# A first expert tile gathered, turned and partly multiplied earlier, inside attention

## Chip, cores and metric

One core of a Trainium2 chip runs the whole program: linear attention, a top-1 mixture of experts (MoE) and a dense gated layer (FFN), in float32. The metric is device time in microseconds (us). The kernel before takes 884.85 us, the median of three runs (881.26 to 886.94).

## What is computed

The reference, cut to its core:

```python
# q, k, v: 4 batches x 8 heads x 576 x 64;  w_phi: 64 x 128
proj = x @ w_phi;  proj = proj - max(abs(proj), -1)
phi(x) = concat(exp(proj), exp(-proj))
kv = phi(k).T @ v;  z = phi(k).sum(2)
attn = (phi(q) @ kv) / (phi(q) @ z + 1e-6)
x = attn as 2304 tokens x 512
e = argmax(x @ w_gate);  g = max softmax(x @ w_gate) * sigmoid(x @ w_output_gate)[e]
x[tokens of e] = g * (relu(x @ w1[e]) @ w2[e])      # 8 experts, 512 -> 1024 -> 512
h = x @ w_in;  out = (h * sigmoid(h)) @ w_out        # 512 -> 2048 -> 512
```

## The kernel before, in words

**Attention** runs in eight units u = 0 to 7, one per pair of heads and half of the tokens (two batches, 1152 tokens, nine tiles of 128). `attention()` writes the order out by hand and the engines keep it: PE (TensorE), DVE (VectorE), ACT (ScalarE) and POOL (GpSimd) execute in that order; only SP's DMA queue is ordered by the scheduler. A unit projects q in three groups (L122), reduces and subtracts the maxima on DVE (L127, L128), adds up kv (L148), copies kv out on ACT (L153), turns q through PSUM (L165) and takes exponentials on ACT (L167, L168), and then attends in three groups g (L184, divided on DVE in L189 to L191), among them the projection of the next unit's k. Small parts are hung in at numbered places n = 0 to 6 of a unit by `other(u, n)`. Units 4 to 7 also load the first expert's weights: the expert that the first half of the tokens chose most often is known in unit 4, and `first_expert(1)` fetches one 128x512 piece into a staging tile `wst` (two rooms), casts it to the high part on ACT (L256) and subtracts for the low part on POOL (L257). There are sixteen pieces, eight each of w1 and w2. All matmuls of the experts and the FFN take a high and a low part of each operand, three matmuls for one product.

**The first tile** is 416 rows of that expert, all of the first half of the tokens. After attention's last q is turned, DVE works out the slots of these tokens (`early_slots`, L465 to L482), nine small matmuls and DVE make a list of tokens (`early_tokens`, L489 to L492), POOL gathers the rows from DRAM (L687) and scales them (L704), and PE turns them (L725) into `xh` and `xl` (L727 ACT, L728 DVE). `gate(1, ...)` meanwhile turns the second half's x (L204), forms logits (L216) and adds them up (L226, L227), and `choose()` picks the experts. PSUM pools in attention: `pj` two tiles of two banks, `pv` one bank, `pm` three.

**The experts.** `Moe.run()` does tile 0 first: eight hidden blocks of twelve matmuls of 416 columns (`first_early`, L789), with the second half's slots (L438 to L441, `route.slots`) after two of them; then `route.tokens` (L489), the gather for tile 1, `route.weights` (some thirty small DVE instructions, L552 to L591), and four output products d = 0 to 3 of 24 matmuls (L826), with `side()` and the turn of tile 1 (L725) after d = 2. Tiles 1 onwards hold 256 rows, or 128 by another branch of the program (`first_small`, L763, `second_small`, L774), depending on how full an expert's last tile is; `way(t, ...)` branches at run time. New expert weights are converted by ACT and DVE (L671, L672) when a tile starts a new expert.

**Side work.** The FFN's weights arrive as float64. Eight of their pieces are converted during the expert tiles, `side_work(i)`: one ACT and six DVE instructions and another ACT and DVE pair (L939 to L970). Before, piece 0 goes into tile 0, pieces 1 and 2 into tile 1, 3 into tile 3, 4 into tile 5, 5 and 6 into tile 6, 7 into tile 7. The FFN follows, on PE alone as its path (L1051, L1072).

Of the kernel before, what the change touches and what calls it, by code (L numbers as in the profile page):

```python
# [21 lines left out]
NF = 128  # L22
# [3 lines left out]
UT = NT // 2  # L26
# [48 lines left out]
def attention(tc, c, k, qT, kT, v, w_phi, w_gate, w_ogate, w1, w2, w, xs, route, early_tile):  # L75
# [5 lines left out]
    xp = c.enter_context(tc.tile_pool(name="a_x", bufs=1))  # L81
    sm = c.enter_context(tc.tile_pool(name="a_s", bufs=4))
    ep = c.enter_context(tc.tile_pool(name="a_e", bufs=1))
    lc = c.enter_context(ExitStack())
    ld = lc.enter_context(tc.tile_pool(name="a_ld", bufs=1))
    pj = c.enter_context(tc.tile_pool(name="a_pj", bufs=2, space=PSUM))
# [25 lines left out]
    def project(u, nm, g):  # L112

        if g == 0:
            st["d" + nm, u] = ep.tile([128, UT, 2, NF], F32, name="d" + nm)
# [12 lines left out]
        V.tensor_tensor(  # L128
            out=d[:, 3 * g:3 * g + 3].rearrange("p t j f -> p j t f"), in0=p, in1=mx.to_broadcast([128, 2, 3, NF]), op=ALU.subtract
        )  # L130

    def exp_k(u, a, z):
        if a == 0:
            st["E", u] = ep.tile([128, UT, 2, 2, NF], F32, name="E")
# [134 lines left out]
    load(0, "k")  # L269
    load(0, "q")  # L270
    load_v(0)
# [5 lines left out]
    for u in range(NU):  # L277
# [24 lines left out]
        kv(u, 1, 1, 1)  # L302
        turn_q(u, 4)
        other(u, 6)
        if u == H // 2 + 1:
            route.ranks(0, pm.tile([128, 512], F32, name="pm"), sm.tile([128, UT * NE], F32, name="rtmp", bufs=1))
        if not last:
            load(u + 1, "q")
            load_v(u + 1)
        else:  # L310
            first_expert(1)
            lc.close()
            tile0 = early_tile()
        for g in range(NG):
            if not last:
                for p in ((0, 1), (), (2,))[g]:
                    project(u + 1, "k", p)
            attend(u, g)
            if not last:
                exp_k(u + 1, 3 * g, 3 * g + 3)  # L320
# [6 lines left out]
            if last:  # L327
                if g < 2:
                    tile0[g](pm)
                else:  # L330
                    tile0[2]()
                gate(1, (0, 3, 10)[g])
# [277 lines left out]
class Moe:  # L610
# [15 lines left out]
    def open(self, c):  # L626
        tc = self.tc
        sp = c.enter_context(tc.tile_pool(name="m_s", bufs=1, reuse_waits="tile"))
        pt, ph, py = (c.enter_context(tc.tile_pool(name=n, bufs=1, space=PSUM, reuse_waits="tile")) for n in ("m_pt", "m_ph", "m_py"))
        self.hh, self.hl = (sp.tile([128, FC, T0], F32R, name=n) for n in ("hh", "hl"))  # L630
        self.y = [sp.tile([128, KC * TW], F32R, name=n) for n in ("yph", "ypl")]
        self.hs = sp.tile([128, FE], F32, name="hs")
        self.turned = self.ring(pt, "pt", [128, 512], 2)
        self.hidden = self.ring(ph, "ph", [128, 2, TW], 4)
        self.result = self.ring(py, "py", [128, 2, TW], 2)
# [148 lines left out]
    def hidden_block(self, p, f, n):  # L784
        nc, w = self.nc, self.w
        for kc in range(KC):
            fs = slice(kc * FE + f * 128, kc * FE + (f + 1) * 128)
            for i, (a, b) in enumerate((("w1h", self.xh), ("w1h", self.xl), ("w1l", self.xh))):
                nc.tensor.matmul(p, w[a][:, fs], b[:, kc, 0:n], start=kc == 0 and i == 0, stop=kc == KC - 1 and i == 2)  # L789

    def first_early(self, blocks):
        nc = self.nc
        for f in blocks:
            p = self.hidden[f % 4].rearrange("p a n -> p (a n)")[:, 0:T0]
            self.hidden_block(p, f, T0)
            h = self.hs[:, f % 2 * 512:f % 2 * 512 + T0]
            nc.scalar.activation(h, p, AF.Relu)
            nc.scalar.copy(self.hh[:, f, :], h)
            nc.gpsimd.tensor_sub(self.hl[:, f, :], h, self.hh[:, f, :].bitcast(F32))

    def first(self, t):
        nc = self.nc
# [25 lines left out]
    def second_early(self, side, turn):  # L828

        banks = [*self.result, *self.hidden[2:4]]  # L830
        for d in range(KC):
            p = banks[d].rearrange("p a n -> p (a n)")[:, 0:T0]
            for f in range(FC):
                self.products(p, f, d, T0, f == 0, f == FC - 1)
            if d == 2:
                side()
                turn()
            self.leave(p.unsqueeze(1), d % 2 * T0)
            self.store(0, slice(d, d + 1), T0, d % 2 * T0)

# [8 lines left out]
    def run(self, route, side_load, side_work, after):  # L849
        tc, nc = self.tc, self.nc  # L850
        side_load(0)
        side_load(1)
        self.first_early((0, 1))
        route.slots(self.turned[0])
        self.first_early(range(2, FC))
        route.tokens(self.turned[1])
        self.gather(1)
        self.scale(1)
        self.gather(2)
        route.weights()  # L860
        self.refill(0, "w1")
        self.new_first(1)

        def side():
            self.refill(0, "w2")
            side_work(0)

        self.second_early(side, lambda: self.turn(1))
# [235 lines left out]
def build(tc, qT, kT, v, w_phi, w_gate, w_ogate, w1, w2, w_in, w_out, out, dbg=None):  # L1104
    nc = tc.nc
    with ExitStack() as c:
# [11 lines left out]
        with ExitStack() as e:  # L1118
            with ExitStack() as m:
# [4 lines left out]
                def early_tile():  # L1124
                    xp = m.enter_context(tc.tile_pool(name="m_x", bufs=1, side="left", reuse_waits="tile"))
                    mo.open_x(xp)
                    route.open(m.enter_context(tc.tile_pool(name="r_s", bufs=1, side="left", reuse_waits="tile")))

                    def tokens(pp):
                        route.early_tokens(pp.tile([128, 512], F32, name="pm"))  # L1130
                        mo.gather_early()

                    def turn(h, pp):
                        mo.turn_early(h, pp.tile([128, 512], F32, name="pm"))

                    return lambda pp: route.early_slots(), tokens, mo.scale_early, turn

                with ExitStack() as a, tc.using_default_side("right"), tc.manual_schedule(engines={ENG.PE, ENG.DVE, ENG.Activation, ENG.Pool}):
                    attention(tc, a, k, qT, kT, v, w_phi, w_gate, w_ogate, w1, w2, w, xs, route, early_tile)
# [105 lines left out]
```

## Time and profile before

| | us |
|---|---|
| median of 3 runs | 884.85 |
| lowest, highest | 881.26, 886.94 |
| the profiled execution: its own time | 886.65 |
| its span, first to last instruction | 884.5 |
| PE busy in the span | 835.2 |
| DVE, ACT, POOL busy | 503.4, 359.8, 151.6 |

A row of a timeline gives the start in the span, the duration, engine, line, operation, what it writes and reads, how many were merged, and in brackets the idle time just before it with what ended it. PE's loads of weights overlap its matmuls. Matmuls are pipelined, so 0.35 us of one matmul is a latency, and the time between two starts is what it costs.

### The profile page before, as it was taken

How to read it: one execution, taken by the hardware profiler on the slowest of the kernel's cores; microseconds unless marked ns; L12 is line 12 of the kernel's file. 1: busy time of each engine (PE TensorE's matmuls, PEld its weight loads, DVE VectorE, ACT ScalarE, POOL GpSimd, SP SyncE). 2: the span in 40 equal slices, each digit the busy share in tenths (PEclk: the TensorE clock that was granted, in tenths of full speed). 3: DMA queues.
4: the chain of work that ended last, by engine and by line, in shares of the span. 5: the costliest groups of instructions: out<-in, count | busy, mean ns of one | idle time of the engine just before them, and what ended most of it. 6: DMA issues, size and time to landing. Idle time of an engine off the chain costs nothing. (4 is left out here: it accounts for less than half of the span.)

```text
span 884.5 us, 19046 instructions
## 1 busy us (share of the span) xinstructions
PE 835.2 (94%) x7812; PEld 763.8 (86%) x7812; DVE 503.4 (57%) x872; ACT 359.8 (41%) x641; POOL 151.6 (17%) x139
## 2 busy tenths in 40 slices
PE   7999998789889999998998999999999999999997
PEld 6888787669878989988998999999999999999996
DVE  5777577447666867666253888888423323232322
ACT  4556566443346665225153545544222222222220
POOL 0000024446422322201260101000002101010001
PEclk9999999999989999999999999999999999999999
DMA  4444356333857798326552855731023120210000
GB/s 143 150 131 127 91 167 186 91 101 106 311 176 250 264 295 301 122 74 210 151 162 83 236 168 168 225 107 49 1 72 100 44 72 36 55 41 13 6 31 36
DMA packets 59217, 113.96 MB, mean 129 GB/s; under 512 B 7056, under 2 KB 47120, under 8 KB 57312
## 3 DMA queue, kind: packets, MB, share of 16 engines
q1 hardware_dynamic: 42640, 81.10, 28.6%
q0 software_dynamic: 16464, 31.33, 12.5%
q8 instruction: 75, 1.23, 0.6%
q14 instruction: 38, 0.31, 0.1%
HBM read 91.79 MB, written 20.62 MB: 127 GB/s over the span
## 5 line engine op out<-in xcount | busy, mean ns | idle before, releaser
L1054 DVE TENSOR_TENSOR g<-fph,g 128x384 f32<-128x384 f32 x96 | 53.5, 557 | 150.8 <-ACT g L1053 150.5
L1053 ACT ACTIVATE g<-fph 128x384 f32<-128x384 f32 x96 | 47.2, 492 | 199.0 <-PE fph L1051 198.9
L789 PE MATMUL ph<-xh,w1h 128*128 128x256 f32 (+1 forms) x256 | 75.1, 293 | 2.2 <-DVE lg L227 1.1
L1055 ACT CAST gh<-g 128x384 fp32r<-128x384 f32 x96 | 49.4, 514 | 64.7 <-DVE g L1054 64.7
L789 PE MATMUL ph<-xh,w1l 128*128 128x256 f32 (+1 forms) x256 | 74.7, 292 | 0.0
L789 PE MATMUL ph<-xl,w1h 128*128 128x256 f32 (+1 forms) x256 | 74.5, 291 | 0.0
L826 PE MATMUL py<-hh,w2h 128*128 128x256 f32 (+1 forms) x240 | 69.9, 291 | 4.6 <-ACT hh L807 3.0
L1058 DVE TENSOR_TENSOR gl<-g,gh 128x384 fp32r<-128x384 f32 x96 | 53.4, 557 | 36.5 <-ACT gh L1055 36.5
L826 PE MATMUL py<-hl,w2h 128*128 128x256 f32 (+1 forms) x240 | 69.1, 288 | 0.7 <-DVE hl L808 0.7
L826 PE MATMUL py<-hh,w2l 128*128 128x256 f32 (+1 forms) x240 | 69.1, 288 | 0.0
L1051 PE MATMUL fph<-yh,i0h 128*128 128x384 f32 x192 | 65.6, 342 | 0.7 <-PEq L908 0.7
L1051 PE MATMUL fph<-yh,i0l 128*128 128x384 f32 x192 | 65.4, 341 | 0.0
L1051 PE MATMUL fph<-yl,i0h 128*128 128x384 f32 x192 | 65.1, 339 | 0.0
L127 DVE TENSOR_REDUCE pmx<-pj 128x6 f32<-128x768 f32 x48 | 45.6, 949 | 32.8 <-PE pj L122 32.8
L985 POOL DMA_DIRECT2D yh<-yTh x12 | 9.3, 776 | 281.3 <-PE fph L1051 228.7
L704 POOL TENSOR_SCALAR xg<-xg 128x512 f32<-128x512 f32 (+1 forms) x28 | 52.4, 1878 | 27.5 <-DMA xg<-xs,tok 27.3
L1072 PE MATMUL fpo<-o0l,gh 128*128 128x512 f32 x144 | 57.0, 396 | 0.0
L1072 PE MATMUL fpo<-o0h,gh 128*128 128x512 f32 x144 | 56.7, 394 | 0.0
L1072 PE MATMUL fpo<-o0h,gl 128*128 128x512 f32 x144 | 56.7, 394 | 0.0
L122 PE MATMUL pj<-wphi,raw 64*64 64x128 f32 x1152 | 44.6, 292 | 10.3 <-PE pj L122 5.3
L789 PEld LDWEIGHTS ph<-xh,w1h 128*128 128x128 f32 x256 | 48.9, 191 | 3.2 <-issue 2.2
L826 PEld LDWEIGHTS py<-hh,w2h 128*128 128x128 f32 x240 | 46.0, 192 | 5.5 <-ACT hh L807 3.2
(267 smaller groups left out, 2172.5 us busy)
## 6 DMA issues: line engine op xcount, KB each, us to landing
w1s<-in_w SPq DMA_DIRECT2D x7, 2048.0 KB, 8.1
w2s<-in_w SPq DMA_DIRECT2D x7, 2048.0 KB, 9.5
yh<-yTh POOLq DMA_DIRECT2D x12, 768.0 KB, 5.0
yl<-yTl POOLq DMA_DIRECT2D x12, 768.0 KB, 7.7
raw<-in_w_in SPq DMA_DIRECT2D x16, 512.0 KB, 5.6
raw<-in_w_out SPq DMA_DIRECT2D x16, 512.0 KB, 3.6
v<-in_v SPq DMA_DIRECT2D x8, 650.0 KB, 3.9
raw<-in_k SPq DMA_DIRECT2D x24, 192.0 KB, 4.3
```

The source lines that it names most:

```text
L122: nc.tensor.matmul(ps[c:c + 64, j, i * 128:(i + 1) * 128], t[h, i * 128 + c:i * 128 + c + 64], wphi[h, :], start=True, stop=True)
L127: V.tensor_reduce(mx, p, AX.X, ALU.max, apply_absolute_value=True)
L704: self.nc.gpsimd.tensor_scalar(x[:, 0:DM], x[:, 0:DM], x[:, DM:DM + 1], None, op0=ALU.mult)
L789: nc.tensor.matmul(p, w[a][:, fs], b[:, kc, 0:n], start=kc == 0 and i == 0, stop=kc == KC - 1 and i == 2)
L826: self.nc.tensor.matmul(p, self.w[a][:, fs], b[:, f, 0:n], start=start and i == 0, stop=stop and i == 2)
L985: self.nc.gpsimd.dma_start(out=y, in_=yT[:, :, ch * CN:(ch + 1) * CN])
L1051: nc.tensor.matmul(p, a[:, kc, fs], b[:, kc, :], start=kc == 0 and n == 0, stop=kc == KC - 1 and n == 2)
L1053: nc.scalar.activation(g, p, AF.Sigmoid)
L1054: V.tensor_mul(g, p, g)
L1055: nc.scalar.copy(gh, g)
L1058: V.tensor_sub(gl, g, gh.bitcast(F32))
L1072: nc.tensor.matmul(p, a[:, s], b[:, f, :], start=q < 2 and f == 0 and n == 0, stop=done and n == 2)
```

## The change

The first tile's slots are worked out in unit 5 at n = 3, its list of tokens and its gather stand at n = 6 of unit 5, its scaling at n = 1 of unit 6, and its four turns at n = 0 to 3 of unit 7; `route.ranks` moves from behind unit 5's n = 6 to its n = 0. Hidden block 0 is put ahead of the last unit's attend groups and blocks 1, 2 and 3 among the gate steps behind them; the blocks write to `pj` tiles. `wst` gets four rooms. `dk` and `E` move to a pool that is closed before the last attend, where the hidden tiles are then placed. In tile 0, `route.tokens` and the gather follow product d = 0, `route.weights` follows d = 1, side work and the turn of tile 1 follow d = 2. Side pieces now go: 0 in tile 0, 1 in tile 1, 2 in tile 3, 3 in tile 5, 4 and 5 in tile 6, 6 and 7 in tile 7.

```diff
@@ attention()
-            t = sm.tile([128, 512], F32, name="wst", bufs=2)
+            t = sm.tile([128, 512], F32, name="wst", bufs=4)
...
+        if u == H // 2 + 1:
+            if n == 0:
+                st["tile0"] = early_tile(pm)
+                route.ranks(0, pm.tile([128, 512], F32, name="pm"), sm.tile([128, UT * NE], F32, name="rtmp", bufs=1))
+            elif n == 3:
+                st["tile0"].slots()
+            elif n == 6:
+                st["tile0"].tokens()
         if u > H // 2 and n in (1, 3, 5, 6):
             first_expert(1)
+        if u == H // 2 + 2 and n == 1:
+            st["tile0"].scale()
+        if (u, n) in TURNS:
+            st["tile0"].turn(TURNS.index((u, n)))
...
+    TURNS = [(NU - 1, n) for n in range(4)]
...
-    tile0[3](0, pm)
-    tile0[3](1, pm)
-    gate(1, 1)
-    tile0[3](2, pm)
-    tile0[3](3, pm)
...
+    st["tile0"].open()
+    block(0)
+    for g in range(NG):
+        attend(u, g)
+        first_expert(1)
+    store_x(bp, hp * 128, st["x", bp][:, :, hp * 128:(hp + 1) * 128])
+    gate(1, 6)
+    block(1)
+    gate(1, 8)
+    block(2)
     gate(1, 1)
     decide(1)
+    block(3)
@@ Moe.run()
-        self.first_early((0, 1))
         route.slots(self.turned[0])
-        self.first_early(range(2, FC))
-        route.tokens(self.turned[1])
-        self.gather(1)
-        self.scale(1)
-        self.gather(2)
-        route.weights()
...
+        self.first_early(range(FC // 2, FC))
+
+        def between(d):
+            if d == 0:
+                route.tokens(self.turned[1])
+                self.gather(1)
+                self.scale(1)
+                self.gather(2)
+            elif d == 1:
+                route.weights()
+                self.refill(0, "w1")
+                self.new_first(1)
+            elif d == 2:
+                self.refill(0, "w2")
+                side_work(0)
+                self.turn(1)
...
             if t == 1:
                 side_work(1)
-                side_work(2)
...
-            for i in {3: (3,), 5: (4,), 6: (5, 6), 7: (7,)}.get(t, ()):
+            for i in {3: (2,), 5: (3,), 6: (4, 5), 7: (6, 7)}.get(t, ()):
```

On DVE at the end of attention, the kernel before had the slots of the first tile (`slot` to `rr`) between two groups of the last attend (`den`, `x`):

```order
L191 TENSOR_TENSOR x<-pm,den 128x3x128
L465 CAST slot<-rank 128x9
L468 TENSOR_SCALAR hi<-slot 128x9
L469 TENSOR_SCALAR lo<-slot 128x9
L473 TENSOR_TENSOR mlo<-lo,col 128x1152
L501 TENSOR_TENSOR eq_2851<-hi,tcol 128x36
L502 TENSOR_TENSOR eq_2851<-eq_2851,oh 128x36
L481 TENSOR_SCALAR rr_2852<-eq_2851,row 128x9x4
L482 TENSOR_TENSOR rr_2852<-eq_2851,tcol 128x9x4
L189 TENSOR_SCALAR den<-pm 128x6
```

In the changed kernel the same eight stand in unit 5 behind the last subtraction for q (`dq`), with the list of tokens (`tok`) behind them and unit 6's first k (`pmx`, `dk`) next:

```order
L130 TENSOR_TENSOR dq<-pj,pmx 128x2x3x128
L482 CAST slot<-rank 128x9
L485 TENSOR_SCALAR hi<-slot 128x9
L486 TENSOR_SCALAR lo<-slot 128x9
L490 TENSOR_TENSOR mlo<-lo,col 128x1152
L518 TENSOR_TENSOR eq_2023<-hi,tcol 128x36
L519 TENSOR_TENSOR eq_2023<-eq_2023,oh 128x36
L498 TENSOR_SCALAR rr_2024<-eq_2023,row 128x9x4
L499 TENSOR_TENSOR rr_2024<-eq_2023,tcol 128x9x4
L508 COPY tokf_2193<-pm 128x8
L509 SCALAR_TENSOR_TENSOR tok_96<-tokf_2193 128x4
L129 TENSOR_REDUCE pmx<-pj 128x6
```

The eight have left the last attend and stand two units earlier.

On PE in unit 7, between the projections of q (`pj<-wphi,raw`) and the turns of q (`pm<-ident,dq`), before:

```order
L148 MATMUL pv<-v_2511,E 64x130 x2
L148 MATMUL pv<-v_2511,E 64x65 x16
L148 MATMUL pv<-v_2511,E 64x130 x2
L148 MATMUL pv<-v_2511,E 64x65 x16
L122 MATMUL pj<-wphi,raw 64x128 x12
L148 MATMUL pv<-v_2511,E 64x130 x2
L148 MATMUL pv<-v_2511,E 64x65 x8
L165 MATMUL pm<-ident,dq 128x128 x8
```

and now, with the turns of the first tile's rows (`pm<-ident,xg`) among them:

```order
L150 MATMUL pv<-v_2555,E 64x65 x8
L743 MATMUL pm<-ident,xg 128x128 x4
L150 MATMUL pv<-v_2555,E 64x65 x8
L150 MATMUL pv<-v_2555,E 64x130 x2
L150 MATMUL pv<-v_2555,E 64x65 x8
L743 MATMUL pm<-ident,xg 128x128 x4
L150 MATMUL pv<-v_2555,E 64x65 x8
L124 MATMUL pj<-wphi,raw 64x128 x12
L743 MATMUL pm<-ident,xg 128x128 x4
L150 MATMUL pv<-v_2555,E 64x130 x2
L150 MATMUL pv<-v_2555,E 64x65 x8
L167 MATMUL pm<-ident,dq 128x128 x8
```

Three turns of 128 rows stand ahead of the first turn of q, and the fourth (32 rows) behind it.

On ACT at the start of tile 1, before, two side pieces (`mag`, `i0h`) stand ahead of the tile's own results (`hh`):

```order
L939 ACTIVATE mag<-raw 128x512
L966 CAST i0h<-val 128x512
L939 ACTIVATE mag<-raw 128x512
L966 CAST i0h<-val 128x512
L638 TENSOR_LOAD full
L880 COMPARE_AND_BRANCH
L807 ACTIVATE hh<-ph_3168 128x2x256
```

and now one:

```order
L959 ACTIVATE mag<-raw 128x512
L986 CAST i0h<-val 128x512
L656 TENSOR_LOAD full
L900 COMPARE_AND_BRANCH
L827 ACTIVATE hh<-ph_3234 128x2x256
```

The second pair has gone to tile 3's side piece and so on, up to tile 7, which now has two.

## Rows read from the trace of the kernel before

**Rows 1.** The page: busy us, share of the span, instructions of each engine.

```profile
PE 835.2 (94%) x7812; PEld 763.8 (86%) x7812; DVE 503.4 (57%) x872; ACT 359.8 (41%) x641; POOL 151.6 (17%) x139
```

**Rows 2.** Windows: length, PE, PEld, DVE, ACT, POOL busy, granted clock, DMA share, GB/s.

```profile
170.00:180.00 10.00, 6.09 (x77) 5.25 (x77) 3.67 (x13) 2.77 (x5) 5.82 (x6) 0.83 0.30 86
```

**Rows 3.** Timeline of PE, unit 6's attend and attention's end.

```profile
146.73 3.10 PE L184 MATMUL pm<-kv,eq 128*64 128x65 f32 x96
...
166.05 2.79 PE L184 MATMUL pm<-kv,eq 128*64 128x65 f32 x88 [1.31 <-ACT kv L153]
171.82 0.38 PE L489 MATMUL pm<-rr,mlo 128*128 128x8 bf16 x9 [2.99 <-DVE rr L482]
172.06 2.60 PE L204 MATMUL pm<-ident,x 128*128 128x128 f32 x12
174.59 2.40 PE L184 MATMUL pm<-kv,eq 128*64 128x65 f32 x48
...
180.06 0.85 PE L216 MATMUL pm<-xT,wg 128*32 128x384 f32 x8 [2.04 <-DVE x L191]
...
189.28 0.43 PE L789 MATMUL ph<-xh,w1h 128*128 128x416 f32 x1 [1.11 <-DVE lg L227]
```

**Rows 4.** Waits of PE: us in total, times, longest us.

```profile
PE pv L148 <- ACT kv L153: 2.3, 2, 1.2
```

**Rows 5.** Timelines of DVE, ACT, POOL and SP's queue in units 5 to 7 and after.

```profile
126.10 0.23 DVE L449 TENSOR_TENSOR rtmp<-pm,oh 128x72 f32<-128x72 f32 x1 [3.35 <-PE pm L441]
...
168.38 0.99 DVE L465 CAST slot<-rank 128x9 int32<-128x9 f32 x1
...
158.14 0.62 ACT L256 CAST w2h<-wst 128x512 fp32r<-128x512 f32 x1 [2.30 <-DMA wst<-in_w]
...
173.23 1.16 POOL L687 DMA_INDIRECT xg<-xs,tok  x1 [3.89 <-DVE tok L492]
...
178.12 6.21 POOL L704 TENSOR_SCALAR xg<-xg 128x512 f32<-128x512 f32 x4
...
146.01 0.43 SPq L109 DMA_DIRECT2D v<-in_v  x1
```

**Rows 6.** Groups by line: the first tile's turns on PE (busy us, mean ns).

```profile
L725 PE MATMUL pm<-ident,xg 128*128 128x128 f32 (+1 forms) x16 | 2.0, 263 | 0.2 <-issue 0.2
```

**Rows 7.** Timeline of PE, tile 0 from the slots to tile 1.

```profile
194.51 0.44 PE L789 MATMUL ph<-xh,w1h 128*128 128x416 f32 x1
...
208.20 0.70 PE L489 MATMUL pt<-rr,mlo 128*128 128x64 bf16 x18
...
227.74 0.28 PE L789 MATMUL ph<-xh,w1h 128*128 128x256 f32 x1
```

**Rows 8.** Timeline of DVE, tile 0: list of tokens, weights, side piece, turn.

```profile
208.93 0.23 DVE L491 COPY tokf<-pt 128x64 f32<-128x64 f32 x1 [3.28 <-PE pt L489]
...
216.75 0.23 DVE L591 TENSOR_SCALAR coff<-coff,taken 128x16 int32<-128x16 f32 x1
...
219.14 0.43 DVE L949 TENSOR_SCALAR mag<-mag 128x512 f32<-128x512 f32 x1
...
224.78 1.29 DVE L728 TENSOR_TENSOR xl<-pt,xh 128x512 fp32r<-128x512 f32 x2 [0.44 <-ACT xh L727]
```

**Rows 9.** Timeline of PE and ACT, tiles 1 to 4.

```profile
240.79 0.62 ACT L966 CAST i0h<-val 128x512 fp32r<-128x512 f32 x1 [4.49 <-DVE val L963]
...
242.93 0.38 PE L826 MATMUL py<-hh,w2h 128*128 128x256 f32 x1 [2.95 <-ACT hh L807]
...
260.58 0.47 PE L763 MATMUL ph<-w1h,xh 128*128 128x512 f32 x1 [3.62 <-ACT w2h L671]
...
277.92 0.38 PE L789 MATMUL ph<-xh,w1h 128*128 128x256 f32 x1 [0.19 <-issue]
...
301.40 0.39 PE L763 MATMUL ph<-w1h,xh 128*128 128x512 f32 x1
```

**Rows 10.** DMA queues from 257 to 259 us: packets, MB, share of 16 engines.

```profile
q8 instruction: 1, 0.02, 2.7%
```

More of the change, by code (lines that the diff above doesn't have):

```diff
@@ L83, in attention @@
     ep = c.enter_context(tc.tile_pool(name="a_e", bufs=1))
+    kc = c.enter_context(ExitStack())
+    ek = kc.enter_context(tc.tile_pool(name="a_k", bufs=1))
     lc = c.enter_context(ExitStack())
@@ L114, in project @@
         if g == 0:
-            st["d" + nm, u] = ep.tile([128, UT, 2, NF], F32, name="d" + nm)
+            st["d" + nm, u] = (ek if nm == "k" else ep).tile([128, UT, 2, NF], F32, name="d" + nm)
         d, t = st["d" + nm, u], st.pop(("raw", nm, u, g))
@@ L133, in exp_k @@
         if a == 0:
-            st["E", u] = ep.tile([128, UT, 2, 2, NF], F32, name="E")
+            st["E", u] = ek.tile([128, UT, 2, 2, NF], F32, name="E")
         E, d = st["E", u], st["dk", u]
@@ L304, in attention @@
         other(u, 6)
[L305 to L310, printed above, removed]
+        if last:
             first_expert(1)
             lc.close()
-            tile0 = early_tile()
+            kc.close()
+            break
+        load(u + 1, "q")
+        load_v(u + 1)
         for g in range(NG):
-            if not last:
-                for p in ((0, 1), (), (2,))[g]:
-                    project(u + 1, "k", p)
+            for p in ((0, 1), (), (2,))[g]:
+                project(u + 1, "k", p)
             attend(u, g)
-            if not last:
-                exp_k(u + 1, 3 * g, 3 * g + 3)
+            exp_k(u + 1, 3 * g, 3 * g + 3)
             if u == H // 2 and g == 1:
@@ L326, in attention, with block @@
                 gate(0, 2)
[L327 to L332, printed above, removed]
-        store_x(bp, hp * 128, st["x", bp][:, :, hp * 128:(hp + 1) * 128])
-    tile0[3](0, pm)
-    tile0[3](1, pm)
-    gate(1, 1)
-    tile0[3](2, pm)
-    tile0[3](3, pm)
+        store_x(bp, hp * 128, st["x", bp][:, :, hp * 128:(hp + 1) * 128])
+    def block(f):
+        if f % 2 == 0:
+            st["free"] = pj.tile([128, 2, 512], F32, name="pj")
+        st["tile0"].block(f, st["free"][:, f % 2, 0:T0])
+    st["tile0"].open()
[8 more added lines that the diff above has]
+    block(2)
     gate(1, 1)
     decide(1)
+    block(3)
 def choose(nc, sp, k, lg, route, bp, scale):
@@ L624, in open_x, with open_s @@
         self.xh, self.xl = (sp.tile([128, KC, T0], F32R, name=n) for n in ("xh", "xl"))
[L626 to L629, printed above, removed]
+    def open_s(self, sp):
         self.hh, self.hl = (sp.tile([128, FC, T0], F32R, name=n) for n in ("hh", "hl"))
@@ L632, in open @@
         self.hs = sp.tile([128, FE], F32, name="hs")
+    def open(self, c):
+        tc = self.tc
+        pt, ph, py = (c.enter_context(tc.tile_pool(name=n, bufs=1, space=PSUM, reuse_waits="tile")) for n in ("m_pt", "m_ph", "m_py"))
         self.turned = self.ring(pt, "pt", [128, 512], 2)
@@ L789, in hidden_block, with block_early @@
                 nc.tensor.matmul(p, w[a][:, fs], b[:, kc, 0:n], start=kc == 0 and i == 0, stop=kc == KC - 1 and i == 2)
+    def block_early(self, f, p):
+        nc = self.nc
+        self.hidden_block(p, f, T0)
+        h = self.hs[:, f % 2 * 512:f % 2 * 512 + T0]
+        nc.scalar.activation(h, p, AF.Relu)
+        nc.scalar.copy(self.hh[:, f, :], h)
+        nc.gpsimd.tensor_sub(self.hl[:, f, :], h, self.hh[:, f, :].bitcast(F32))
     def first_early(self, blocks):
-        nc = self.nc
         for f in blocks:
[L794 to L799, printed above, removed]
+            self.block_early(f, self.hidden[(f + 2) % 4].rearrange("p a n -> p (a n)")[:, 0:T0])
     def first(self, t):
@@ L826, in products, with second_early @@
             self.nc.tensor.matmul(p, self.w[a][:, fs], b[:, f, 0:n], start=start and i == 0, stop=stop and i == 2)
-    def second_early(self, side, turn):
+    def second_early(self, between):
         banks = [*self.result, *self.hidden[2:4]]
@@ L834, in second_early @@
                 self.products(p, f, d, T0, f == 0, f == FC - 1)
-            if d == 2:
-                side()
-                turn()
+            between(d)
             self.leave(p.unsqueeze(1), d % 2 * T0)
@@ L852, in run @@
         side_load(1)
-        self.first_early((0, 1))
         route.slots(self.turned[0])
-        self.first_early(range(2, FC))
-        route.tokens(self.turned[1])
-        self.gather(1)
-        self.scale(1)
-        self.gather(2)
-        route.weights()
[L861 to L868, printed above, removed]
+        self.first_early(range(FC // 2, FC))
[13 more added lines that the diff above has]
+                self.turn(1)
+        self.second_early(between)
         def one(t):
@@ L1122, in build, with __init__, pool, bank @@
                 mo = Moe(tc, k, r, w, {"w1": w1, "w2": w2}, xs, yT)
[L1124 to L1130, printed above, removed]
-                        mo.gather_early()
-                    def turn(h, pp):
-                        mo.turn_early(h, pp.tile([128, 512], F32, name="pm"))
-                    return lambda pp: route.early_slots(), tokens, mo.scale_early, turn
+                class Early:
+                    def __init__(self, pp):
+                        self.pp = pp
+                        mo.open_x(self.pool("m_x"))
+                        route.open(self.pool("r_s"))
+                    def pool(self, name):
+                        return m.enter_context(tc.tile_pool(name=name, bufs=1, side="left", reuse_waits="tile"))
+                    def bank(self):
+                        return self.pp.tile([128, 512], F32, name="pm")
+                    def slots(self):
+                        route.early_slots()
+                    def tokens(self):
+                        route.early_tokens(self.bank())
+                        mo.gather_early()
+                    def scale(self):
+                        mo.scale_early()
+                    def turn(self, h):
+                        mo.turn_early(h, self.bank())
+                    def open(self):
+                        mo.open_s(self.pool("m_s"))
+                    def block(self, f, p):
+                        mo.block_early(f, p)
                 with ExitStack() as a, tc.using_default_side("right"), tc.manual_schedule(engines={ENG.PE, ENG.DVE, ENG.Activation, ENG.Pool}):
-                    attention(tc, a, k, qT, kT, v, w_phi, w_gate, w_ogate, w1, w2, w, xs, route, early_tile)
+                    attention(tc, a, k, qT, kT, v, w_phi, w_gate, w_ogate, w1, w2, w, xs, route, Early)
                 ep = e.enter_context(tc.tile_pool(name="f_e", bufs=1, side="right", reuse_waits="tile"))
```

## The prediction

> **What bounds the kernel now.** I read the page first: PE is busy for 835.2 of 884.5 us, 94% of the span [rows 1], so a change pays only where PE stands still or runs slowly, or where it moves that. The FFN at the end is a closed row of matmuls that the change doesn't touch; it starts earlier by whatever PE gains before it. Then I went through the windows of 10 us for places where PE's busy time falls: in 170 to 180 us it is 6.09 of 10, and the granted clock 0.83 [rows 2]. The timeline of PE there names the waits one by one [rows 3]: 1.31 for the last kv copy, 2.99 for the slots' `rr` on DVE, 2.04 behind the last attend, 1.11 for the last logits before the first hidden block; in sum 7.45 us. [...] The second place is tile 1: from 227.74 [rows 7] to the end of its work, 3.62 before 260.58, are 29.2 us, while tile 3, with the same matmuls, takes 301.40 - 277.92 = 23.5 [rows 9]. Between them stands a wait of 2.95 for ACT's `hh`, and ACT was busy with a side piece: its `i0h` of 240.79 had itself waited 4.49 for DVE [rows 9]. Last, PE stands 3.62 before tile 2, at a branch.
>
> **Part by part, against the profiled execution** (886.65 us, 1.8 above the median of the runs shown).
>
> *End of attention.* The chain of slots, list, gather, scale and turn leaves it. Hidden block 0 (one block costs (208.20 - 194.51)/6 = 2.28 us [rows 7]) covers the 1.31; the 2.99 is gone with the slots; blocks 1 and 2 stand where PE waited for the logits' copies; block 3 stands ahead of the second half's slots while `choose` finds the experts. The blocks themselves are only moved. So 7.45 of waits, 1.95 of slow clock, 2.0 of turns [rows 6] and the 0.24 of the list's matmuls (171.82 to 172.06 [rows 3]) leave: 11.6. Against it: three `pm` rooms serve nine turns of x, and ACT now copies them between the blocks' `relu` and cast, which are ahead of the copies in its queue; and DVE must have `choose` done within one block where it had two. The trace before doesn't show that interleaving. Bounds are 0 (each copy lies beside a block) and 3.7, half of the waits there were; I take 1.0, nearer to nothing because a block is longer than any of the copies. Net -10.6, between -11.6 and -7.9.
>
> *Units 5 to 7, which receive the chain.* Slots: 168.38 to 171.82 on DVE, 3.4 us [rows 5, 3], and, as an estimate from the 0.24 of the nine matmuls, some 0.8 with the two DVE instructions behind and the handing over. DVE has 3.35 idle at that place of unit 5 [rows 5], so 0.9 comes out, and what is late is unit 6's first k; bounds 0 and 3.4. Turns: 2.0 on PE in unit 7, which has little idle time; four `xl` on DVE go into a queue that is full there, and the fourth turn needs the `pm` room that the third `xl` frees behind the last subtraction for q: +0.8, bounds 0 and 2. Staging: twice, in units 6 and 7, PE waits for the kv copy, 2.3 together [rows 4], and ACT stood just before that copy in a cast that waited 2.30 for the `wst` DMA [rows 5]; with four rooms that DMA is issued some pieces ahead, so -2.3 (bounds -2.3 and 0). Gather and scale are POOL time, about 4.9 (173.23 to 178.12) and 6.2 [rows 5], beside pieces of w1 and w2 that now have four rooms; I cost them at nothing. If that cover were gone, SP's queue would be late; that is the third rival. Sum +1.4, between -0.3 and +7.4.
>
> *Tile 0.* From the list's matmuls to tile 1, 208.20 to 227.74, are 19.5 us [rows 7]: 0.6 for the list, about 1.0 for the turn of two row blocks, four products of 4.5. Now product 0 goes ahead of the list, so four blocks and one product (13.7) cover the slots' DVE chain, as six blocks (13.7) did; but only 15.0 are left between list and tile 1. DVE's work in that stretch isn't less: from 208.93 to the end of `xl` at 226.07 [rows 8], that is up to 17.9 after the list's matmuls began: the weights' small instructions until 217, the side piece from 219.14, then `xl`. An instruction or two of waiting for ACT falls away, so 17.5. Tile 1's second matmul needs `xl`; PE waits 2.5 us there, where it waited for nothing. Behind this `xl` stand the products' `ypl` and then side piece 1. Bounds: 0, if the changed order lets DVE start early, and 4.5, one product. A wait of 2.99 was followed by the slow clock [rows 3]; half of 1.95 is put down for that, +1.0.
>
> *Tile 1.* One side piece instead of two: DVE is done with it before tile 1's first results are all there, the 2.95 goes, and with it the slow stretch behind. What takes its place is tile 3's shape: 23.5 instead of 29.2, -5.7; bounds -5.7 and -3.0 (the wait alone). The piece goes to tile 3 in exchange for another, and at the end tile 7 gets one more; tiles 3 and 7 have the same matmuls and DVE idle beside them, so nothing.
>
> *Tile 2's branch:* unchanged. The row names ACT's `w2h` as what ended it [rows 9], but in tile 4 the same matmul starts without a wait though the same conversion runs; in 257 to 259 us one packet of instructions is fetched [rows 10]. So I read it as the fetch of the branch's code, which the change doesn't move. [...]
>
> Sum: -10.6 + 1.4 + 2.5 + 1.0 - 5.7 = -11.4. 886.65 - 11.4 = 875.25; taken off the median instead, 884.85 - 11.4 = 873.4, which is the forecast.
>
> **Rivals.** *First, the branch too.* If the fetch comes in time, as in tile 4, another 3.62 and a slow stretch like the 1.95 go: 873.4 - 5.6 = 867.8. For it: tile 4; against it: the same code is reached in the same way.
>
> *Second, DVE becomes the bound.* Every link that leaves PE's end of attention lands in DVE's queue in units 5 and 7, and tile 0 gives it 4.5 us less. If the slots come out whole (+2.5 more), the turns' `xl` by their bound (+1.2 more) and the chain before tile 1 by 4.5 (+2.0 more), 5.7 are given back: 879.1, within 1%. For it: DVE is busy through most of each unit; against it: the idle 3.35 stands right where the slots are put.
>
> *Third, slower, by SP's queue.* SP issues in order, a `wst` load only when POOL has freed a room, and unit 7's v (issued at 146.01 [rows 5]) stands behind such loads. The gathers and scales put 4.9 + 6.2 = 11.1 in front of POOL's pieces. If nothing of that were hidden, PE would stand for 11.1 in units 6 and 7 and run slowly after it (1.95): 873.4 + 13.0 = 886.4, slower than before. It decides if v is issued later than about 150 us; four rooms and two units between them speak against it.
>
> **How the numbers follow.** Forecast as summed 0.57 (its own range 870 to 877), branch too 0.13, DVE 0.25, SP's queue 0.05. The bounds of the parts would allow 862 to 885; nearly all of that at the ends needs several together, so 866 to 880 holds 8 in 10. About 1%, 8.85 us, is what a measurement tells from no change: faster than 876.0 are most of the first case and the second, 0.68; slower than 893.7 only an SP queue worse than priced, 0.03; the rest 0.29.
>
> **What would show it.** Right: no wait of PE for `rr` or for `lg` before the first block; no kv wait of about 1.1 in units 6 and 7; the first FFN matmul some 11 us earlier; tile 1 at about 24 us, with a wait of 2 to 3 for `xl` or `xh` just before it; tile 2's 3.6 still there. Wrong: gaps of PE in units 5 to 7 that end on DVE or on a DMA for v, k or q; waits for ACT's `xT` or `lt` among the gate steps of more than 3 in sum; tile 1's start less than 4 us earlier than 227.74.

## The result and the profile after

The changed kernel takes 873.71 us, the median of four runs (872.32 to 875.18), beside 885.89 for the kernel before on the same chip: ratio 0.9883, 95% interval 0.9858 to 0.9909, faster by 1.2%. A second measurement, below, gave 0.990 (0.9867 to 0.9934), 8.4 us by its medians. The forecast was 873.4 us.

In the profiled execution PE's busy time fell by 5 us [rows 1], and the window in which the kernel before did 6.09 us of work at a clock of 0.83 [rows 2] is nearly full. The page's line, and the window (length, busy time of PE, PEld, DVE, ACT, POOL, granted clock, DMA share, GB/s):

```profile
PE 830.3 (95%) x7812; PEld 758.6 (87%) x7812; DVE 503.9 (58%) x872; ACT 359.1 (41%) x641; POOL 149.4 (17%) x139
```

```profile
170.00:180.00 10.00, 9.39 (x127) 8.02 (x123) 2.52 (x8) 5.03 (x10) 1.17 (x2) 1.00 0.20 62
```

Two marks of the kernel before, from PE's timeline: unit 7's last turns of q, and the FFN's first matmul.

```profile
163.90 0.44 PE L165 MATMUL pm<-ident,dq 128*128 128x128 f32 x2
...
475.56 0.41 PE L1051 MATMUL fph<-yh,i0h 128*128 128x384 f32 x1 [0.73 <-PEq L908]
```

The same marks in the changed kernel, and between them what answers to [rows 3, 7, 9]: waits among the gate steps, the second half's slots (L455), the list (L506), tile 1's first two matmuls, tile 2's first.

```profile
165.04 0.44 PE L167 MATMUL pm<-ident,dq 128*128 128x128 f32 x2
...
173.28 1.50 PE L206 MATMUL pm<-ident,x 128*128 128x128 f32 x12 [0.15 <-DVE x L193]
...
179.68 0.66 PE L206 MATMUL pm<-ident,x 128*128 128x128 f32 x4 [0.46 <-ACT xT L209]
...
186.40 0.45 PE L807 MATMUL pj<-xh,w1h 128*128 128x416 f32 x1 [0.34 <-ACT hs L813]
188.78 0.50 PE L455 MATMUL pt<-oh,ones 128*128 128x80 bf16 x9
...
203.06 0.70 PE L506 MATMUL pt<-rr,mlo 128*128 128x64 bf16 x18
...
218.21 0.38 PE L807 MATMUL ph<-xh,w1h 128*128 128x256 f32 x1
219.34 0.38 PE L807 MATMUL ph<-xl,w1h 128*128 128x256 f32 x1 [0.74 <-DVE xl L746]
...
247.06 0.76 PE L781 MATMUL ph<-w1h,xh 128*128 128x512 f32 x1 [4.21 <-ACT w2h L689]
...
461.94 0.60 PE L1071 MATMUL fph<-yh,i0h 128*128 128x384 f32 x1 [0.72 <-PEq L928]
```

Read as differences, the 13.6 us between the two FFN rows split so: +1.1 up to the turns of q (165.04 against 163.90), made of +1.8 in units 5 to 7 (63.3 us from unit 4's last turn of q, at 101.78, instead of 61.5 from 102.40) and -0.6 ahead of them, where the change does nothing; -9.6 from there to tile 1 at work (219.34 - 165.04 = 54.3, where the kernel before needed 227.74 - 163.90 = 63.8, with 0.1 to its second matmul); -5.7 in tile 1 (219.34 to 242.85, which is 4.21 before 247.06: 23.5 us instead of 29.2); +0.6 at tile 2's branch (4.21 instead of 3.62); the rest up to the FFN is equal within 0.1 (214.88 and 214.98 us).

### The profile page after: what moved, and what is told of

Same layout as the page of the kernel before. It is cut to its first block, busy times and chain, and to the rows that moved or that the text cites. A ratio compares the mean times of both kernels' runs of the same rounds, so it can differ in the third digit from the quotient of the medians.

```text
span 870.8 us, 19045 instructions
## 1 busy us (share of the span) xinstructions
PE 830.3 (95%) x7812; PEld 758.6 (87%) x7812; DVE 503.9 (58%) x872; ACT 359.1 (41%) x641; POOL 149.4 (17%) x139
## 5 line engine op out<-in xcount | busy, mean ns | idle before, releaser
L807 PE MATMUL ph<-xh,w1h 128*128 128x256 f32 (+1 forms) x240 | 68.8, 287 | 1.2 <-ACT yph L840 0.7
L807 PE MATMUL ph<-xl,w1h 128*128 128x256 f32 (+1 forms) x240 | 68.3, 285 | 0.7 <-DVE xl L746 0.7
L807 PE MATMUL ph<-xh,w1l 128*128 128x256 f32 (+1 forms) x240 | 68.3, 284 | 0.0
L722 POOL TENSOR_SCALAR xg<-xg 128x512 f32<-128x512 f32 (+1 forms) x28 | 49.8, 1785 | 31.1 <-DMA xg<-xs,tok 31.0
L124 PEld LDWEIGHTS pj<-wphi,raw 64*64 64x64 f32 x1152 | 34.3, 142 | 16.3 <-issue 7.4
L150 PEld LDWEIGHTS pv<-v,E 128*64 128x64 f32 x1152 | 40.9, 140 | 7.7 <-issue 6.7
```

The costliest lines, as they stand in the source:

```text
L124: nc.tensor.matmul(ps[c:c + 64, j, i * 128:(i + 1) * 128], t[h, i * 128 + c:i * 128 + c + 64], wphi[h, :], start=True, stop=True)
L150: nc.tensor.matmul(pv[f:f + 64, s, o:o + n], E[:, i, j, s, f:f + 64], v1[:, c:c + n], start=i == 4 and s == 0, stop=i == 8 and s == 1,)
L722: self.nc.gpsimd.tensor_scalar(x[:, 0:DM], x[:, 0:DM], x[:, DM:DM + 1], None, op0=ALU.mult)
```

## Experiments

Ratios are to the kernel before, run beside each; 0.001 is 0.9 us. Where nothing else is said, a difference to the changed kernel is taken to 0.9883; to its second ratio, 0.990, it is 1.5 us smaller.

**The pieces, both ways.** In the changed kernel, put back:

```diff
             if t == 1:
                 side_work(1)
+                side_work(2)
-            for i in {3: (2,), 5: (3,), 6: (4, 5), 7: (6, 7)}.get(t, ()):
+            for i in {3: (3,), 5: (4,), 6: (5, 6), 7: (7,)}.get(t, ()):
```

> The changed kernel with the FFN pieces where they stood before (tile 1 converts pieces 1 and 2 again). My theory (term D of the sum): tile 1 is held up by the second piece alone, so its 23.5 to 24.6 us go back to about 29 and the whole is 5.7 us slower than the changed kernel, about 879.4 us, with a wait of PE for hh of about 3 us in tile 1 and a stretch at the lower clock behind it. Rival: tile 1 became shorter because DVE's queue ahead of it is different now, and the piece is harmless: 0 to 2 us slower.

Measured 0.9944 (0.9921 to 0.9966), 5.4 us over the changed kernel's 0.9883. PE's timeline:

```profile
233.00 0.56 PE L846 MATMUL py<-hh,w2h 128*128 128x256 f32 x1 [3.21 <-ACT hh L827]
...
250.32 0.77 PE L781 MATMUL ph<-w1h,xh 128*128 128x512 f32 x1 [2.21 <-ACT w2h L689]
```

The wait for `hh` is back, and tile 1 takes 30.6 us from its second matmul. Two of the 7.0 lost there don't count, because tile 2's wait shrinks from 4.21 to 2.21. The opposite edit, in the kernel before:

> The kernel before with only the FFN pieces moved as in the change. My theory: the term D stands by itself, so tile 1 falls from 29.2 to 23.5 us and the whole is 5.7 us faster than before (ratio about 0.9936). Rival: the wait for hh in tile 1 is tied to before's order of tile 0, and goes only in part: 0 to 3 us.

Measured 0.9946 (0.9924 to 0.9967), 4.8 us faster than before.

```profile
225.13 0.28 PE L789 MATMUL ph<-xh,w1h 128*128 128x256 f32 x1
...
252.56 0.77 PE L763 MATMUL ph<-w1h,xh 128*128 128x512 f32 x1 [3.90 <-ACT w2h L671]
...
270.96 0.38 PE L789 MATMUL ph<-xh,w1h 128*128 128x256 f32 x1 [0.18 <-issue]
```

Tile 1 takes 23.5 us here too. Tile 2's wait is 0.3 longer and its work 1.1 (18.4 against 277.92 - 260.58 = 17.3 [rows 9]). So the term stands by itself, about 5 us after what tile 2 takes back.

**Staging rooms.**

```diff
-            t = sm.tile([128, 512], F32, name="wst", bufs=4)
+            t = sm.tile([128, 512], F32, name="wst", bufs=2)
```

> The changed kernel with two staging rooms instead of four. My theory (part of term A): PE waits again for the kv copy behind ACT's cast, twice about 1.1 us, so +2.3 us against the changed kernel (about 876). Rival one: the chain of gather and scale in front of POOL's pieces makes it worse with two rooms, v of unit 7 is issued late and PE stands for it: +5 or more. Rival two: the waits had gone for another reason, as the order of the casts: 0.

Measured 0.995 (0.9928 to 0.9971): 5.9 us over 0.9883, 4.4 over 0.990. ACT's cast stands in unit 6 for its DMA, PE behind it for the copy, and then PE runs at a granted clock of 0.50 (timelines of ACT and PE, and a window):

```profile
138.69 0.62 ACT L258 CAST w1h<-wst 128x512 fp32r<-128x512 f32 x1 [1.96 <-DMA wst<-in_w]
```

```profile
139.64 0.91 PE L150 MATMUL pv<-v,E 128*64 128x130 f32 x20 [2.44 <-ACT kv L155]
```

```profile
140.60:144.00 3.40, 3.40 (x36) 3.07 (x38) 0.00 (x0) 2.39 (x5) 3.40 (x4) 0.50 0.59 197
```

The mechanism is the one of [rows 4, 5], with its whole weight in unit 6 and a slow stretch that I hadn't priced: 2.44 and some 1.7, an estimate (half of the 3.40 at 0.50). The first half of my first rival holds too: POOL issues the gather until 131.57, frees rooms with its next two pieces until 134.09, and only at 134.12 does SP issue the load that this cast waits for. Its second half doesn't: no gap of PE in units 6 and 7 ends on v. Then both small edits, alone, in the kernel before:

> The kernel before with the two small edits alone: four staging rooms and the FFN pieces moved, nothing of tile 0's chain. My theory: the two terms add up, -2.3 (kv copies in units 6 and 7) and -5.7 less the 0.3 to 1.3 that the kernel before with the pieces alone gave back at tile 2: -6.7 to -8.0 us against before, ratio 0.991 to 0.9925, more than half of the whole change's gain. Rival: the kv waits of the kernel before aren't due to the staging rooms (there nothing but the pieces is in POOL's queue): -4.4 to -5.7.

Measured 0.9916 (0.9896 to 0.9936), 7.4 us faster than before. No wait for the kv copy is left in units 6 and 7, while the end of attention is as it was:

```profile
164.54 2.79 PE L184 MATMUL pm<-kv,eq 128*64 128x65 f32 x88 [1.30 <-ACT kv L153]
169.49 0.38 PE L489 MATMUL pm<-rr,mlo 128*128 128x8 bf16 x9 [2.17 <-DVE rr L482]
```

In this profile units 5 to 7 take 61.4 us, as before (61.5): two pauses of PE with nothing waited for, 2.33 before 114.99 (0.88 at that place in the kernel before) and 1.43 before 151.41, stand against the kv waits that went. So what the rooms give in this kernel rests on the ratios, whose intervals overlap (this run's and the one with the pieces alone).

Two edits of a line or two give most of the whole gain. The long one, tile 0's chain and order, adds some 1.5 to 3 us to them by the ratios, which isn't clear of noise (0.9896 to 0.9936 overlaps both intervals of the changed kernel), though 9.6 leave the stretch from the turns of q to tile 1; the last section has a place where some of that is lost.

**Blocks or chain.** The chain stays in units 5 to 7, the four blocks go back behind attention:

```diff
-    block(0)
...
-    gate(1, 6)
-    block(1)
-    gate(1, 8)
-    block(2)
-    gate(1, 1)
+    gate(1, 15)
     decide(1)
-    block(3)
@@ Moe.run()
+        self.first_early((0, 1))
         route.slots(self.turned[0])
-        self.first_early(range(FC // 2, FC))
+        self.first_early(range(2, FC))
```

> The changed kernel with hidden blocks 0 to 3 of tile 0 back behind attention (0 and 1 ahead of the second half's slots, as before), so only the chain of slots, list, gather, scale and turns stays in units 5 to 7. My theory (term B split in two): the wait of 2.99 us for rr, the slow stretch behind it (1.95), the turns (2.0) and the list's 0.24 stay gone, because they belong to the chain; what the four blocks cover comes back: 1.31 for the kv copy, 2.04 behind the last attend, 1.11 for the logits, 4.5 us in sum, less the 0.95 of small new waits that the interleaving brought: +3.5 us against the changed kernel, and up to 1.95 more if one of the waits is followed by the lower clock. Rival: without the slots in its queue DVE is through with the gate's steps early, and the blocks cover nothing: 0 to 1 us.

Measured 0.9901 (0.988 to 0.9921), no different from the changed kernel. PE's timeline:

```profile
167.48 0.44 PE L167 MATMUL pm<-ident,dq 128*128 128x128 f32 x2
...
169.43 4.19 PE L186 MATMUL pm<-kv,eq 128*64 128x65 f32 x136 [1.13 <-ACT kv L155]
174.79 1.50 PE L206 MATMUL pm<-ident,x 128*128 128x128 f32 x12 [0.15 <-DVE x L193]
...
182.54 0.55 PE L228 MATMUL pm<-ident,lt 128*128 128x128 f32 x3 [0.65 <-ACT lt L220]
187.47 0.50 PE L449 MATMUL pt<-oh,ones 128*128 128x80 bf16 x9
...
222.52 0.38 PE L801 MATMUL ph<-xl,w1h 128*128 128x256 f32 x1 [0.82 <-DVE xl L740]
```

From the turns of q to tile 1 at work are 55.0 us, 0.7 more than with the blocks. Only the 1.31 for the kv copy came back (as 1.13); the 2.04 behind the last attend is 0.15, and the 1.11 for the logits hasn't returned, only 0.65 at an earlier step. So these two waits weren't for lack of other work on PE. DVE's rows of the kernel before show what they were:

```profile
178.93 0.17 DVE L189 TENSOR_SCALAR den<-pm 128x6 f32<-128x6 f32 x1 [6.01 <-PE pm L204]
...
187.98 0.89 DVE L728 TENSOR_TENSOR xl<-pm,xh 128x512 fp32r<-128x512 f32 x2 [0.79 <-ACT xh L727]
188.79 0.35 DVE L227 TENSOR_REDUCE lg<-pm 128x48 f32<-128x192 f32 x1
```

The last `lg` (the 1.11) stood in DVE's queue behind the first tile's `xl`. The last attend's `den` (the 2.04) had itself waited for PE, which had the list's matmuls and twelve turns of x ahead of that attend [rows 3]; in the changed kernel and in this run all gate steps stand behind the attends. The slots' instructions account for the 2.99. My theory fell and the rival holds, though not by the slots only; moving the gate steps wasn't tried by itself.

**Tile 0's order.** The list, weights and first conversion ahead of the products again, as before:

```diff
+        route.tokens(self.turned[1])
+        self.gather(1)
+        self.scale(1)
+        self.gather(2)
+        route.weights()
+        self.refill(0, "w1")
+        self.new_first(1)
         def between(d):
-            if d == 0:
...
-            elif d == 2:
+            if d == 2:
```

> The changed kernel with tile 0's list, weights and first conversion ahead of the four products, as before, while four blocks stay in attention. My theory (term C): the slots' chain on DVE, which one block more than four has to cover (13.7 us of PE's work in either kernel), is covered by 9.1 us only, so PE waits up to 4.5 us at the list's matmuls and may run slowly behind it; in exchange the 0.74 us for xl before tile 1 goes. In sum +3 to +6 us against the changed kernel. Rival: DVE is through with the slots earlier than that, and the list may stand anywhere: 0 to 1 us, or a little faster than the changed kernel because nothing waits for xl.

Measured 0.9927 (0.9907 to 0.9946). PE waits once, and not for `xl`:

```profile
201.29 0.68 PE L506 MATMUL pt<-rr,mlo 128*128 128x64 bf16 x18 [2.09 <-DVE rr L499]
```

From the slots to tile 1 at work that is 1.1 us more than in the changed kernel's profile (189.27 to 220.94, against 188.78 to 219.34), so the wait came at half of its 4.5, and the stage is near my rival's 0 to 1. The ratio says 3.9 us (2.4 to 0.990). The FFN starts 3.1 us later: 0.5 of that comes ahead of the turns of q, and 1.7 behind tile 2's start, where the granted clock is 0.50 in 388.40 to 391.80, which the changed kernel's first profile hasn't there. So the ratio isn't the price of the order alone. The list could start 11.4 us after the slots' matmuls (9.3 of blocks and the wait), sooner than the 13.7 that I took as its cover. Then the turn ahead of the piece:

```diff
+                self.turn(1)
                 side_work(0)
-                self.turn(1)
```

> The changed kernel with the turn of tile 1's rows ahead of the FFN piece in tile 0 instead of behind it. My theory (term C): the 0.41 to 0.82 us that PE waits for xl before tile 1 is DVE's queue alone, in which the piece (4.95 us) stands ahead of xl; with xl first the wait goes and the piece lies beside product 3 and tile 1: -0.4 to -0.8 us, nothing new in tile 1. Rival: the piece now delays the yph and ypl of product 3 and, in ACT's and DVE's queues, tile 1's first hidden results, so PE waits for hh or hl in tile 1 as it did in the kernel before: +1 to +4 us.

Measured 0.9878 (0.9854 to 0.9903), no different from the changed kernel.

```profile
218.89 0.28 PE L807 MATMUL ph<-xh,w1h 128*128 128x256 f32 x1
...
247.83 0.77 PE L781 MATMUL ph<-w1h,xh 128*128 128x512 f32 x1 [5.41 <-ACT w2h L689]
```

The wait for `xl` is gone and tile 1 takes 23.5 us, but tile 2's wait grew from 4.21 to 5.41: from the slots to tile 2 it is 58.3 us in either kernel. What is gained ahead of that branch is partly waited away at it.

**Tile 2's branch.** Matmuls that never execute, in the branch for small tiles of tile 1 (36 or 72), move the rest of PE's program. The changed kernel ran beside them:

```diff
     def first_small(self, t):
+        if t == 1:
+            for _ in range(36):
+                nc.tensor.matmul(...)
```

> The changed kernel itself, as the yardstick on the chip of the other three: the same waits as in its first profile (0.74 for xl before tile 1, about 4.2 at tile 2's branch, 1.5 at tile 8's), and a ratio to before of about 0.988.

Measured 0.990 (0.9867 to 0.9934), with 0.41 for `xl`, 4.84 at tile 2 and 1.91 at tile 8.

> The changed kernel with 36 matmuls added to the branch of tile 1 for small tiles, which isn't taken here: nothing more is executed, but all of PE's program behind it lies 72 instructions later. My theory (term E): the wait before tile 2 is the fetch of the branch's code. PE passes a prefetch hint for the branch one stage ahead of it, and the wait comes where, between hint and branch, the program goes over from one instruction packet to the next (a packet is 16.4 KB in the rows: 1.23 MB in 75). [...] With 36 matmuls more it is so for 2, 4 and 8: the 4.2 and 1.5 stay and tile 4 gets a wait of 2 to 4 us, so 2 to 4 us slower than the changed kernel. [...] Rival: the wait is for ACT's w2h, as the row names it: then no wait changes in any of the three shifts, and the time is the changed kernel's.

Measured 0.9901 (0.9868 to 0.9934).

```profile
246.64 0.39 PE L784 MATMUL ph<-w1h,xh 128*128 128x512 f32 x1
...
290.13 0.77 PE L784 MATMUL ph<-w1h,xh 128*128 128x512 f32 x1 [4.16 <-ACT w2h L689]
```

> As the run before, with 72 matmuls in the branch that isn't taken (144 instructions). By the same count hint and branch of tiles 2 and 8 now lie in one packet and those of tile 4 don't: my theory expects no wait at tile 2 (4.2 before) and tile 8 (1.5), and one of 2 to 4 us at tile 4; in sum -1.5 to -3.5 us against the changed kernel, and another 1.7 (a stretch of 3.4 us at half the clock) if the lower clock behind tile 2's wait goes and none comes behind tile 4's. Rival (ACT's w2h): nothing changes.

Measured 0.989 (0.9859 to 0.9921).

```profile
246.04 0.39 PE L784 MATMUL ph<-w1h,xh 128*128 128x512 f32 x1
...
386.98 0.36 PE L795 MATMUL py<-w2h,hh 128*128 128x256 f32 x1 [3.43 <-ACT w1h L689]
...
450.85 0.47 PE L784 MATMUL ph<-w1h,xh 128*128 128x512 f32 x1 [2.79 <-ACT w2h L689]
```

> Unexecuted matmuls in three places (72 in tile 1's branch for small tiles, 40 and 80 in the branches of tiles 2 and 4 for full ones, none of which is taken here), so that by my count hint and branch lie in one packet for tiles 2, 4 and 8. My theory expects none of the three waits: -4.2 - 1.5 = -5.7 us against the changed kernel, or -7.4 with the stretch at the lower clock, about 866 to 868 us where the changed kernel takes 873.7. Rival (ACT's w2h): nothing changes. A second rival: a branch that is taken costs its wait at some other tile whatever the places are, then 0 to -3.

Measured 0.9929 (0.9908 to 0.9951).

```profile
256.87 0.38 PE L795 MATMUL py<-w2h,hh 128*128 128x256 f32 x1 [2.80 <-ACT w1h L689]
...
298.12 0.38 PE L795 MATMUL py<-w2h,hh 128*128 128x256 f32 x1 [2.37 <-ACT w1h L689]
```

ACT does the same work in all four, yet the wait leaves tile 2 and goes to tile 4, to tile 8's second stage (1.75 of these 3.43 is a wait for DVE that the changed kernel has too) and the last small tile, or to the second stage of tiles 2 and 4 (with 72, another 1.74 stands inside tile 2's second stage). (That last small tile is tile 11; the expectations call it 12.) So it hangs on where PE's code lies and not on `w2h`: the row names what came last, not what was waited for. The DMA records of the traces bear this out. In all ten executions that wait at tile 2, one packet of instructions (16 KB) starts 2.6 to 2.8 us before PE goes on (at 244.31 in the changed kernel, PE at 247.06), and so it does at tile 4 with 36 (287.51, PE at 290.13). In the four that don't wait at tile 2, the last packet started 3.7 to 8.5 us ahead of it (with 36 at 242.96, PE at 246.64). My count of the places was wrong (with 36, tile 2 should have waited). The last attempt took the place without a wait for each tile from these runs:

```diff
     def first_small(self, t):
+        for _ in range({1: 36, 3: 36, 7: 120}.get(t, 0)):
+            nc.tensor.matmul(...)
```

> The changed kernel with unexecuted matmuls in the branches for small tiles of tiles 1, 3 and 7 (36, 36 and 120, none taken here), which gives tile 2 the place in the program that it had with 36 (no wait seen there), tile 4 the one that it had with 72 (none there), and tiles 8 and 12 those of the three-place run. My theory now, after three shifts in which the waits changed their places but not their sum (6.8 and 7.2 us in the changed kernel, 6.9, 7.6 and 10.7 with the shifts, counted as waits at small tiles with nothing but a branch, an issue gap or a converted weight behind them): the sum can't be placed away; it will be 5 to 8 us again, at other places, and the time within 2 us of the changed kernel. Rival: each branch's wait hangs on its own place alone: nothing at tiles 2 and 4, 1.3 + 2.3 at 8, 1.8 at 12, so 5.4 us or less, and 1.5 to 2 us faster than the changed kernel.

Measured 0.9838 (0.9811 to 0.9865), the lowest ratio of all.

```profile
244.41 0.39 PE L783 MATMUL ph<-w1h,xh 128*128 128x512 f32 x1
...
378.07 1.06 PE L743 MATMUL pt<-ident,xg 128*128 128x128 f32 x8 [1.35 <-issue]
385.84 0.58 PE L794 MATMUL py<-w2h,hh 128*128 128x256 f32 x1 [1.52 <-issue]
...
454.03 0.43 PE L794 MATMUL py<-w2h,hh 128*128 128x256 f32 x1 [2.70 <-issue]
```

Tiles 2 and 4 start without a wait, as in the runs from which their places were taken, so there a branch's wait hangs on its own place. At tiles 8 and 11 the places were those of the three-place run, and the waits weren't the same: 1.52 inside tile 8's second stage for 2.31, and 2.70 in tile 11's second stage for 1.81 in its first. The place alone doesn't fix every wait. The waits that are left make 5.6 us, against 6.8 in the changed kernel (4.21, 1.51 and 1.10). The ratio is some 0.005 lower, more than that explains; it wasn't measured beside the changed kernel, and the intervals overlap a little (0.9858 to 0.9865). It beats the kernel before clearly and the changed one probably, for data that fill the tiles as here.

## Why the prediction was right, step by step

By parts, forecast and measured in the profiles: end of attention -10.6 and -10.8, units 5 to 7 +1.4 and +1.8, tile 0 +3.5 and +1.2, tile 1 -5.7 and -5.6, tile 2's branch 0 and +0.6; -0.6 lies ahead of all of them. That the median came within 0.3 us of 873.4 is luck: the profiles differ by 13.6 us, the medians by 12.2 and those of the second measurement by 8.4, where 11.4 was forecast. The upper bound of the parts, 885, is added up wrong: -7.9 + 7.4 + 4.5 + 1.0 - 3.0 on 884.85 is 886.9; nothing else used it.

- **The end of attention, -10.6: right in sum, wrong in its parts.** From the turns of q to the slots were 193.90 - 163.90 = 30.0 us, now 188.78 - 165.04 = 23.7 with two blocks more: 10.8 less. But "hidden block 0 covers the 1.31", "blocks 1 and 2 stand where PE waited for the logits' copies" was right only in its first half: without the blocks 0.7 us is lost, not 3.5. Nearly all of it went with the chain and the gate steps put behind the attends. The new waits, put at 1.0, are 0.15 + 0.46 + 0.34 = 0.95. The 1.95 of slow clock is an estimate from the trace before: behind the 2.99 the granted clock was 0.50 in 172.91 to 176.32, and about there twelve turns of x took 1.1 us more than at the pace of the first tile's turns, 48 attend matmuls 0.85 more than half of unit 6's 96 [rows 3, 6]. In the changed kernel the granted clock is 1.00 in 164 to 188.
- **Units 5 to 7, +1.4: right in this execution (+1.8), too low as a rule.** Four rooms do end the kv waits, and POOL's gather and scale are hidden by the rooms. But the sum had no term for PE pausing with nothing waited for: with the early chain and four rooms these units took +1.8 to +3.3 us in three profiled executions and +3.9 to +5.6 in seven, as the last section shows. All lie inside the bounds given (-0.3 to +7.4).
- **Tile 0, +2.5 and +1.0: too high.** PE waits 0.74 or 0.41 for `xl`, and no slow clock follows the 0.74 (granted 1.00 in 219.30 to 225.00). DVE's rows answer to [rows 8]:

```profile
203.80 0.23 DVE L508 COPY tokf<-pt 128x64 f32<-128x64 f32 x1 [2.13 <-PE pt L506]
...
211.44 0.23 DVE L608 TENSOR_SCALAR coff<-coff,taken 128x16 int32<-128x16 f32 x1
...
212.93 0.42 DVE L969 TENSOR_SCALAR mag<-mag 128x512 f32<-128x512 f32 x1
...
217.99 1.29 DVE L746 TENSOR_TENSOR xl<-pt,xh 128x512 fp32r<-128x512 f32 x2
```

  From the list's copy to the end of `xl` DVE needs 15.5 us, where it took 17.1. The step that failed is "an instruction or two of waiting for ACT falls away, so 17.5": 0.9 comes out between `coff` and `mag`, where one product's `ypl` is already done; that `ypl` now stands ahead of the weights, whose small instructions ran shorter by as much. The rest is the 0.44 for `xh` that isn't waited and a few instructions that ran shorter.
- **Tile 1, -5.7: right**, in both directions of the test.
- **Tile 2's branch, unchanged: right (4.21 instead of 3.62), and for its reason as far as the runs show it.** The four shifts show code and not ACT, and a packet of instructions starts 2.6 to 2.8 us before the waits at tile 2, and tile 4's with 36, end; the same branch costs 4.21 (changed kernel) or nothing (with 36) by its place alone. That PE waits for this packet is my inference from the two going together. My counts of places for the first three shifts use a number of instructions to a packet that no run shows. What the runs showed in their place: with 36 tile 4 waited 4.16 and tile 2 not at all, with 72 neither did at its start, and with the three places the second stages of tiles 2 and 4 waited 2.80 and 2.37.
- **The rivals.** The branch didn't go. DVE didn't become the bound. SP's queue wasn't late: no gap of PE in units 6 and 7 ends on v.

## What to carry to other kernels

When an engine waits at the end of a stage, ask whose instructions stand in the waited-for queue before filling the gap: taking the first tile's chain out of the end of attention gave 8.8 us up to tile 1 (some 2.2 of it PE's own turns and list, which only moved), the four blocks put in its place 0.7. Try the small edits alone first; here a piece moved by one tile and two more buffers gave 7.4 us, and the long rearrangement little more. A wait at a run-time branch that names an odd producer is tested by moving the code behind it with instructions that never execute, and by looking when the last packet of instructions came.

## What was not expected of the hardware

In unit 6 PE paused without waiting for anything the profile names, in seven of the ten executions that have the early chain and four rooms. All seven ran on two of the chips; two of the other three ran on a third chip, and that of the first measurement isn't known, so the pauses may go with the chip. In the changed kernel's second profile, two of six such pauses, four matmuls and 0.73 us apart, in the attend (PE's timeline, then the window):

```profile
132.09 0.35 PE L186 MATMUL pm<-kv,eq 128*64 128x65 f32 x4 [0.36 <-issue]
132.82 0.35 PE L186 MATMUL pm<-kv,eq 128*64 128x65 f32 x4 [0.38 <-issue]
```

```profile
132.00:136.00 4.00, 2.34 (x42) 1.78 (x46) 1.13 (x5) 2.04 (x3) 3.62 (x4) 1.00 0.93 325
```

Unit 6, from the last turn of q to its own, in us:

| executions | unit 6 |
|---|---|
| before; with late pieces; with two edits | 19.6; 20.0; 18.5 |
| early chain, no pauses: changed, list first, pieces early | 19.3; 19.4; 19.4 |
| early chain, six pauses: changed again, turn first | 21.6; 21.5 |
| the same with a slow stretch behind: four shifts, blocks late | 23.0 to 23.2 |
| early chain, two rooms | 22.7 |

Where the pauses come, unit 6 takes 2 to 4 us more, which the changed kernel's first profile doesn't show and its second does. In one of the slow stretches (the last shift) the granted clock is 0.50:

```profile
133.30:136.70 3.40, 3.40 (x68) 3.07 (x60) 2.64 (x4) 0.41 (x1) 0.81 (x1) 0.50 0.66 202
```

In that part of unit 6 the gather's DMAs, the `wst` loads and the next k and v come together: the DMA share of the window above is 0.93. But crowded DMA queues alone don't make the pauses. In the 4 us that begin 5 us after unit 5's last turn of q, the share is 0.90 to 1.01 in the seven executions that pause and 0.94 to 0.98 in the three that don't. What makes PE pause stays open.

Tile 2's wait also takes back gains made ahead of it (5.41 with the turn first) and gives back losses (2.21 with the early piece), as if part of it ended at a time of its own. That time goes with the packet of instructions: with the turn first it starts at 245.19, 2.8 us after tile 1's last matmul, with the early piece at 247.69, 0.4 ahead of it, and PE goes on 2.6 us after the start in both. What sets the packet's start stays open.
